# Preparation of a state-space filter: its reciprocals spread over more rounds, its low parts on another engine, and a longer pace

## The chip, the cores and the metric

The kernel runs on one core of a Trainium2 chip. The core has TensorE (matmuls, written to PSUM; PE in the profile), VectorE (DVE), ScalarE (ACT), GpSimd (POOL) and SyncE (SP), which mostly issues DMAs. Each engine takes its own instructions strictly in the order of its queue and waits for others by semaphores. The metric is device time in microseconds. Three runs of the kernel before took 731.43 us in the median (729.15 to 732.84).

## The reference

The input `u` is 2048 tokens of 448 channels. It is normalised per token, and three things are added up: the input itself, a long convolution of the normalised input (one filter per channel, given by 256 complex exponentials), and a gated unit with 1792 hidden units.

```python
x = A_u
xn = _layernorm(x, axis=-1)
return x + _A_ref(xn, ...) + _B_ref(xn, B_w_gate, B_w_up, B_w_down)

# _A_ref: filter K from log_A_real, A_imag, C_real, C_imag, log_dt, then a convolution
dt = jnp.exp(log_dt)
A = -jnp.exp(log_A_real) + 1j * A_imag
C = (C_real + 1j * C_imag) * dt[:, None]
P = jnp.exp((A * dt[:, None])[:, :, None] * pos[None, None, :])
K = 2.0 * jnp.einsum("dn,dnl->dl", C, P).real
y = irfft(rfft(u_t, 2 * L) * rfft(K, 2 * L), 2 * L)[:, :, :L]     # plus u * D_skip

# _B_ref
h = sigmoid(x @ w_gate) * (x @ w_up)
return h @ w_down
```

## The kernel before

Two Python generators emit the program side by side: `conv()` for the convolution and `glu()` for the gated unit. Each `yield` gives a number of units; a loop always advances the generator that has done the smaller share of its `total`. So the numbers `WP`, `WX`, `WK`, `WS` and `HOLE` set how much of the gated unit is emitted beside each stretch of the convolution. The order of emission gives priorities to a scheduler, which lays out each engine's queue by a timeline of its own; `hp(...)` raises a priority and `tc.issue_after(...)` keeps an instruction behind another.

The gated unit works in fp32 split in two parts (high and low, type `fp32r`). A slice is one of 14 blocks `f` of 128 hidden units and one of two tiles `t` of 512 tokens of a half; the halves of the tokens come one after the other. A slice has 22 matmuls into two PSUM banks `gu` (L705), a tanh on ScalarE (`th`, L713), `hf` on VectorE, which frees the second bank (L716), its high part `hh` on ScalarE (L721) and low part `hl` on VectorE (L723). In the first half each block also has its weights split: `wh` on ScalarE (L756), `wl` on VectorE (L760), `dh` on ScalarE (L786), `dl` on GpSimd (L787). After two or three blocks come eight groups of matmuls `po` of two or three blocks (L817), each added to `acc` by VectorE (an eviction, L822). `gu` and `po` share four PSUM banks, in turn.

The convolution's head loads and normalises the first 1024 tokens and then prepares the filter's parameters. `prep(pool, h, srcs)` is a generator that handles half the channels (112 partitions, 512 elements); two of them (h = 0, 1) are stepped in turn, one step each per round, with `yield WP` after a round. Its steps:

- the exponential of `log_A_real` and `log_dt` (`exp`, L297 to L310: mostly VectorE),
- modulus and angle of C: the larger part `m3` (L348), its reciprocal in four pieces of 128 (`pieces(m3)`, L314), quotient `w3`, then ScalarE's sign and arctan (L350 to L357),
- 1/(1 + tanh) as `pl`, again `pieces(pl)`, and from it `W1` by transposes on TensorE into `ko` and `kp` (`turn`, L427),
- sine and cosine of the angle, the phases U, V and T (L378 to L404), each in a high part (`high`, ScalarE, L387) and a low part (`low`, GpSimd, L394), all stored to DRAM by `keep` (SP's queue, L383),
- the factors `a3`, `b3` (L411 to L415), turned into `GG`.

In rounds 2 and 3 the loop also emits eight first-stage blocks of the tokens' spectra (`x_spec`: matmuls L278 into `tr`, a copy on ScalarE L289, stores on SP L292). These matmuls are kept behind the newest gated-unit matmul in emission.

Then `kgen` makes the filter in 56 steps of 8 channels: phases loaded back from DRAM into `ph` (`phase_load`, L482), a matmul into `tr` (L532), sines on ScalarE (L540 to L543), magnitudes `me`, `mf` on GpSimd (L498, L510) with powers `pm` on VectorE (L446), the products `Et` and `Ft` on VectorE (L597 to L599), and 64 small matmuls `ko` (L613). Last come the products of the spectra and the way back (`spectra`, from L839), emitted beside the rest of the gated unit.

Of the kernel before, what the change touches and what calls it, by code (L numbers as in the profile page):

```python
# [15 lines left out]
ALU = mybir.AluOpType  # L16
# [5 lines left out]
N = 256  # L22
# [6 lines left out]
NFT = F // 128  # L29
WK = 5.5  # L30
WS = 4.5
HOLE = 6
WS = 4.5
WP = 5
WX = 2
HELD = 9
HP = 300
Y0 = (8, 1)
# [12 lines left out]
NCK = D // DC  # L51
# [77 lines left out]
def s4d_glu_kernel(ctx, tc, io):  # L129
    nc = tc.nc  # L130
    hp = tc.high_priority
    v = nc.vector
# [138 lines left out]
    def row(b, g):  # L271
        return 32 * (b // 4 % 2) + 8 * g + 4 * (b // 8) + b % 4

    def x_first_stage(to, xn, g):

        s = slice(32 * g, 32 * g + 32)
        for i in range(2):
            nc.tensor.matmul(to[64 * i : 64 * i + 64], wx[s], xn[i][s], start=True, stop=True)  # L278

    def x_spec(xn, b0):  # L280

        for p in range(2):
            x1 = slots[("x1a", "x1b", "x1c")[x1s[0] % 3]]
            x1s[0] += 1
            ps = psc[-1].tile([128, 2, 512], F32, name="tr", bufs=1)
            with tc.issue_after(glu_mm[0].ins):
                for j in range(2):
                    x_first_stage(ps[:, j, :D], xn, 2 * p + j)
            nc.scalar.copy(x1, ps[:, :, :D])  # L289
            for i in range(2):  # L290
                r = row(b0 + i, 2 * p)
                nc.sync.dma_start(x1_d[:, r : r + 9 : 8], x1[64 * i : 64 * i + 64])  # L292
            yield WX

    def exp(ex, ki, fr, pl):

        v.tensor_scalar(ex, ex, lim[:CP, 0, 1:2], lim[:CP, 0, 2:3], ALU.min, ALU.max)  # L297
        yield
        nc.scalar.activation(ki, ex, AF.Identity, scale=1.0 / math.log(2.0))
        yield  # L300
        ln2h = 0.693359375
        ln2l = math.log(2.0) - ln2h
        v.scalar_tensor_tensor(fr, ki, -ln2h, ex, ALU.mult, ALU.add)
        v.scalar_tensor_tensor(fr, ki, -ln2l, fr, ALU.mult, ALU.add)
        cs = [1.0 / math.factorial(i) for i in range(8)]
        v.tensor_scalar(pl, fr, cs[7], None, ALU.mult)  # L306
        for i in range(6, 0, -1):
            v.scalar_tensor_tensor(pl, pl, cs[i], fr, ALU.add, ALU.mult)
        v.tensor_scalar(ki, ki, 127.0, 8388608.0, ALU.add, ALU.mult)
        v.scalar_tensor_tensor(ex, pl, 1.0, ki.bitcast(F32), ALU.add, ALU.mult)  # L310

    def pieces(t):
        for i in range(0, 2 * N, 128):
            v.reciprocal(t[:, i : i + 128], t[:, i : i + 128])  # L314


    SF = [CP, 2 * N]
# [15 lines left out]
    def prep(pool, h, srcs):  # L333

        cr, ci, aim, ex = srcs
        new = lambda n, sh=SF, dt=F32: pool.tile(sh, dt, name=n, bufs=2)
        a3, b3, m3, w3, s3 = (new(n) for n in ("a3", "b3", "m3", "w3", "s3"))
        ki, fr, pl = new("ki", [CP, 2 * N + 2], I32), new("fr", [CP, 2 * N + 2]), new("pl", [CP, 2 * N + 2])
        hdt = pool.tile([CP, 2], F32, name="hdt", bufs=2)
        part = lambda t, i: t[:, N * i : N * i + N]  # L340
        dt = lambda i: ex[:, 2 * N + i : 2 * N + i + 1]

        nc.scalar.activation(a3, cr, AF.Abs, scale=lim[:CP, 0, 0:1])
        nc.scalar.activation(b3, ci, AF.Abs, scale=lim[:CP, 0, 0:1])
        yield from exp(ex, ki, fr, pl)
        v.tensor_scalar(hdt, ex[:, 2 * N :], 0.5, None, ALU.mult)
        yield
        v.scalar_tensor_tensor(m3, a3, 1e-37, b3, ALU.max, ALU.max)  # L348
        pieces(m3)
        v.tensor_tensor(w3, a3, b3, ALU.min)  # L350
        v.tensor_tensor(w3, w3, m3, ALU.mult)
        v.tensor_tensor(s3, a3, b3, ALU.subtract)
        nc.scalar.activation(s3, s3, AF.Sign)
        nc.scalar.activation(cr, cr, AF.Sign)
        nc.scalar.activation(w3, w3, AF.Arctan)
        if h == 1:
            nc.scalar.activation(junk[:CP], w3[:, 0:1], AF.Silu)  # L357
        yield

        fr, pl, ki = fr[:, : 2 * N], pl[:, : 2 * N], ki[:, : 2 * N]  # L360
        for i in range(2):
            nc.scalar.activation(part(fr, i), part(ex, i), AF.Tanh, scale=hdt[:, i : i + 1])
        nc.scalar.activation(pl, fr, AF.Identity, bias=one[:CP])
        pieces(pl)
        v.scalar_tensor_tensor(pl, fr, -2.0, pl, ALU.mult, ALU.mult)
        yield
        turn(pl, W1s[0], h)
        v.scalar_tensor_tensor(w3, w3, -math.pi / 4, s3, ALU.add, ALU.mult)
        nc.scalar.activation(m3, w3, AF.Sin, bias=qpi[:CP])
        nc.scalar.activation(s3, w3, AF.Sin, scale=-1.0, bias=qpi[:CP])  # L370
        v.scalar_tensor_tensor(w3, w3, -math.pi / 4, cr, ALU.add, ALU.mult)
        nc.scalar.activation(w3, w3, AF.Identity, bias=hpi[:CP])
        v.tensor_scalar(ci, ci, 0.0, -2.0 / TWO_PI, ALU.is_lt, ALU.mult)
        v.scalar_tensor_tensor(w3, ci, 1.0 / TWO_PI, w3, ALU.add, ALU.mult)
        yield

        for i in range(2):
            v.tensor_scalar(part(fr, i), part(aim, i), 1.0 / TWO_PI, dt(i), ALU.mult, ALU.mult)  # L378
        nc.scalar.copy(ki, fr)
        U, V, T = aim, fr, w3  # L380
        def keep(d, i, src):
            rows = d[2 * CP * h : 2 * CP * h + 2 * CP].rearrange("(t p) i n -> p t i n", t=2)
            nc.sync.dma_start(rows[:, :, i], three(src).bitcast(F32))  # L383

        def high(i, src):
            hi = slots[f"P{i}"][:, h]
            nc.scalar.copy(hi, src)  # L387
            keep((phu_d, phv_d, phv_d)[i], (0, 0, 1)[i], hi)
            if i:
                keep(phh_d, i - 1, hi)  # L390

        def low(i, src):
            lo = src.bitcast(F32R)
            nc.gpsimd.tensor_tensor(lo, src, slots[f"P{i}"][:, h], ALU.subtract)  # L394
            keep((phu_d, phv_d, phv_d)[i], (1, 3, 2)[i], lo)

        v.tensor_tensor(U, fr, ki, ALU.subtract)
        nc.scalar.activation(ki, U, AF.Identity, scale=64.0)
        v.scalar_tensor_tensor(w3, U, 31.5, w3, ALU.mult, ALU.add)
        yield  # L400
        v.scalar_tensor_tensor(V, U, -64.0, ki, ALU.mult, ALU.add)
        v.scalar_tensor_tensor(w3, V, 0.5, w3, ALU.mult, ALU.add)
        nc.scalar.copy(ki, w3)
        v.tensor_tensor(T, ki, w3, ALU.subtract)  # L404
        for i, src in enumerate((U, V, T)):
            high(i, src)
        for i, src in enumerate((U, V, T)):
            low(i, src)
        yield

        v.tensor_tensor(a3, a3, s3, ALU.mult)  # L411
        v.tensor_tensor(b3, b3, m3, ALU.mult)
        v.tensor_tensor(a3, a3, b3, ALU.add)
        for i in range(2):
            v.tensor_scalar(part(a3, i), part(a3, i), 2.0, dt(i), ALU.mult, ALU.mult)  # L415
        yield
        turn(a3, GGs[0], h)
        yield
# [598 lines left out]
    def conv():  # L1017
        with tc.tile_pool(name="psk", bufs=1, space=PSUM) as ps_, tc.tile_pool(
# [9 lines left out]
            with tc.tile_pool(name="pst", bufs=1, side="right", reuse_waits="tile") as pst:  # L1028
# [18 lines left out]
                xns = []  # L1047
# [34 lines left out]
                n = 0  # L1082
                while preps:
                    for p in list(preps):
                        try:
                            with tc.issue_after(hfs[max(0, len(hfs) - LAG)].ins):
                                next(p)
                        except StopIteration:
                            preps.remove(p)
                    yield WP  # L1090
                    n += 1
                    if n in (2, 3):
                        if n == 2:
                            slots["x1c"] = pst.tile([128, 2, D], F32, name="x1c", tag="raw1")
                        for b in range(0, 4, 2):
                            yield from x_spec([xns[n - 2][:, b + i] for i in range(2)], 4 * (n - 2) + b)
            with tc.tile_pool(name="pk", bufs=1, side="right", reuse_waits="tile") as pk:
                yield from kgen(pk)
        yield HOLE
# [8 lines left out]
    xq, psc, raws, acl, marks, slots, pqs = list(x_first), [], [], [], [None, None], {}, []  # L1108
    W1s, GGs, act = [], [], []
    gens = [conv(), glu()]  # L1110
    total = [sum(Y0) + 11 * WP + 8 * WX + 14 + NCK * WK + HOLE + 17 * WS, 2 * (4 + NFT * 14.8) - HELD]
    done = [0.0, 0.0]
    done[0] += next(gens[0])
    held = False
    while any(g is not None for g in gens):
# [3 lines left out]
        i = min(live, key=lambda i: done[i] / total[i])  # L1119
# [33 lines left out]
```

## Time and profile before

| what | value |
|---|---|
| median of three runs | 731.43 us (729.15 to 732.84) |
| the profiled execution's own time | 734.12 us |
| its span, first to last instruction | 732.3 us |
| mean granted TensorE clock | 0.973 |
| DMA | 116.76 MB, mean 159 GB/s |

The profile is of one execution, whose time is the span and 1.8 us around it. Lines of it are read like this: a line of the timeline has start, length, engine, line of the kernel (L705), operation, output and input by the program's names, shape and count, and in brackets how long the engine was idle before it and what ended that. Matmul durations overlap, since they are pipelined; the distance from start to start is what one costs. "SPq" and "ACTq" are DMA issues on SP and ScalarE.

### The profile page before, as it was taken

How to read it: one execution, taken by the hardware profiler on the slowest of the kernel's cores; microseconds unless marked ns; L12 is line 12 of the kernel's file. 1: busy time of each engine (PE TensorE's matmuls, PEld its weight loads, DVE VectorE, ACT ScalarE, POOL GpSimd, SP SyncE). 2: the span in 40 equal slices, each digit the busy share in tenths (PEclk: the TensorE clock that was granted, in tenths of full speed). 3: DMA queues.
4: the chain of work that ended last, by engine and by line, in shares of the span. 5: the costliest groups of instructions: out<-in, count | busy, mean ns of one | idle time of the engine just before them, and what ended most of it. 6: DMA issues, size and time to landing. Idle time of an engine off the chain costs nothing.

```text
span 732.3 us, 19070 instructions
## 1 busy us (share of the span) xinstructions
PE 680.6 (93%) x7780; PEld 535.8 (73%) x7780; DVE 567.3 (77%) x776; ACT 420.8 (57%) x650; POOL 377.3 (52%) x423
## 2 busy tenths in 40 slices
PE   2898799997998999999999999999999999989994
PEld 1665688786876887566878887888877787766783
DVE  5799996799989999998498988986955555654553
ACT  3646364678587778997388678768633312313310
POOL 2120027799887788786557856767843003251001
PEclk9998899999999999997999999999999999999998
DMA  9946328435314544553952322232359999999756
GB/s 202 227 111 199 80 82 276 146 104 186 126 51 154 176 155 136 157 151 120 267 179 98 93 97 96 76 102 96 70 160 294 265 233 239 217 227 250 178 138 162
DMA packets 93287, 116.76 MB, mean 159 GB/s; under 512 B 12177, under 2 KB 81169, under 8 KB 92945
## 3 DMA queue, kind: packets, MB, share of 16 engines
q1 hardware_dynamic: 83888, 95.08, 48.1%
q10 hardware_dynamic: 6736, 14.57, 6.3%
q0 software_dynamic: 2576, 5.90, 3.3%
q8 instruction: 61, 1.00, 0.6%
q14 instruction: 26, 0.20, 0.1%
HBM read 70.75 MB, written 44.76 MB: 158 GB/s over the span
## 4 chain that ended last, share of the span: by engine, by line
PE 60%; DVE 17%; DMA 6%; ACT 6%; issue 5%; SPq 3%; POOL 1%; ACTq 0%; DVEq 0%; POOLq 0%
PE gu L705 23%; PE po L817 15%; PE sp L899 7%; PE ko L613 6%; PE pv L926 4%; PE tr L532 3%; DVE Ft L599 2%; DVE Et L598 2%; DVE Et L597 2%; DVE hl L723 2%; DMA acc_d<-acc 1%; DMA sx<-x_d 1%; DVE wl L760 1%; DVE hf L716 1%; PE kq L558 1%
## 5 line engine op out<-in xcount | busy, mean ns | idle before, releaser
L510 POOL TENSOR_TENSOR me<-me,pm 128x32 f32<-128x32 f32 (+1 forms) x168 | 144.4, 860 | 88.4 <-DVE Et L598 76.3
L510 POOL TENSOR_TENSOR mf<-mf,pm 128x64 f32<-128x64 f32 (+1 forms) x112 | 119.5, 1067 | 4.9
L705 PE MATMUL gu<-xh,wh 128*128 128x512 f32 x336 | 101.1, 407 | 3.0 <-ACT xh L218 2.8
L705 PE MATMUL gu<-xh,wl 128*128 128x512 f32 x336 | 96.1, 394 | 0.0
L705 PE MATMUL gu<-xl,wh 128*128 128x512 f32 x336 | 95.1, 390 | 0.0
L817 PE MATMUL po<-dh,hh 128*128 128x448 f32 x224 | 86.6, 387 | 3.3 <-DVE acc L822 2.5
L597 DVE TENSOR_TENSOR Et<-me,S 128x1024 f32<-128x1024 f32 x56 | 81.6, 1457 | 8.0 <-ACT S L543 4.1
L598 DVE TENSOR_TENSOR Et<-me,S 128x1024 f32<-128x1024 f32 x56 | 79.8, 1425 | 8.2 <-ACT me L523 5.8
L599 DVE TENSOR_TENSOR Ft<-mf,S 128x1024 f32<-128x1024 f32 x56 | 78.9, 1408 | 7.3 <-ACT S L543 4.4
L817 PE MATMUL po<-dl,hh 128*128 128x448 f32 x224 | 84.3, 376 | 0.0
L817 PE MATMUL po<-dh,hl 128*128 128x448 f32 x224 | 83.6, 375 | 0.0
L540 ACT ACTIVATE S<-tr 128x1024 f32<-128x1024 f32 x56 | 57.7, 1030 | 42.7 <-PE tr L532 37.4
L721 ACT CAST hh<-hf 128x512 fp32r<-128x512 f32 x56 | 35.0, 626 | 80.4 <-DVE hf L716 62.8
L705 PEld LDWEIGHTS gu<-xh,wh 128*128 128x128 f32 x336 | 61.8, 191 | 21.7 <-ACT xh L218 4.2
L705 PEld LDWEIGHTS gu<-xh,wl 128*128 128x128 f32 x336 | 63.3, 189 | 15.2 <-DVE pl L306 0.7
L613 PEld LDWEIGHTS ko<-Et,Ft 128*32 128x32 f32 x3584 | 54.1, 111 | 27.4 <-issue 16.6
L705 PEld LDWEIGHTS gu<-xl,wh 128*128 128x128 f32 x336 | 63.1, 188 | 14.1 <-issue 0.7
L613 PE MATMUL ko<-Et,Ft 128*32 128x64 f32 x3584 | 64.2, 222 | 9.0 <-DVE Et L597 4.6
L716 DVE SCALAR_TENSOR_TENSOR hf<-th,gu 128x512 f32<-128x512 f32 x56 | 38.1, 681 | 36.4 <-PE gu L705 27.3
L822 DVE SCALAR_TENSOR_TENSOR acc<-po,acc 128x448 f32<-128x448 f32 x80 | 48.5, 615 | 22.8 <-PE po L817 22.7
L543 ACT ACTIVATE S<-S,hpi 128x1024 f32<-128x1024 f32 x56 | 65.6, 1171 | 0.0
L723 DVE TENSOR_TENSOR hl<-hf,hh 128x512 fp32r<-128x512 f32 x56 | 48.9, 874 | 16.6 <-ACT hh L721 16.6
(196 smaller groups left out, 1293.9 us busy)
## 6 DMA issues: line engine op xcount, KB each, us to landing
sk_d<-sk ACTq DMA_DIRECT2D x14, 512.0 KB
sx<-x_d SPq DMA_DIRECT2D x32, 224.0 KB
skl<-sk_d SPq DMA_DIRECT2D x16, 448.0 KB
vp<-v_d SPq DMA_DIRECT2D x16, 448.0 KB
v_d<-vt SPq DMA_DIRECT2D x62, 112.0 KB
wt_d<-wh SPq DMA_DIRECT2D x9, 512.0 KB
wt_d<-wl SPq DMA_DIRECT2D x9, 512.0 KB
wl<-wt_d SPq DMA_DIRECT2D x9, 512.0 KB
```

The lines of the kernel that those rows point to most:

```text
L510: ins = nc.gpsimd.tensor_tensor(m[:, :, w + a : 2 * w : n], m[:, :, a:w:n], par(base + i).unsqueeze(2).to_broadcast([128, 4 * DC, w // n]) ...
L540: nc.scalar.activation(rows(cs), pv, AF.Abs)
L543: sins[:] = [nc.scalar.activation(cs, cs, AF.Sin, scale=-TWO_PI, bias=hpi)]
L597: v.tensor_tensor(Et[:, :, :, 32:64], two(me[:, :, 32:64]), S[:, 1::-1], ALU.mult)
L598: v.tensor_tensor(Et[:, :, :, 0:32], two(me[:, :, 0:32]), S[:, 1:3, :, ::-1], ALU.mult)
L599: fts[:] = [v.tensor_tensor(Ft, two(mf), S[:, 3:5], ALU.mult)]
L613: nc.tensor.matmul(ko[32 * j : 32 * j + 32, sl], Ft[:, cc, DC * h + 4 * q + j], Et[:, cc, DC * h + 4 * q + j], start=(k == 0), stop=(k == ...
L705: glu_mm[:] = [nc.tensor.matmul(ps, a_, b_, start=(n == 0), stop=(n == len(mm) - 1))]
L723: v.tensor_tensor(hl, hf, hh, ALU.subtract)
L817: glu_mm[:] = [nc.tensor.matmul(po, a_[:, bs], w_, start=(n == 0), stop=(n == 3 * fc - 1))]
L822: v.scalar_tensor_tensor(acc[:, b], po, 0.5, acc[:, b], ALU.mult, ALU.add)
L899: mm = nc.tensor.matmul(to, tb[:kk, t, 64 * c : 64 * c + 64], rhs, start=True, stop=True, skip_group_check=True,)
```

## The change

The diff, line numbers as in the file before:

```diff
-WP = 5
+WP = 70 / 19
@@
-    def pieces(t):
-        for i in range(0, 2 * N, 128):
-            v.reciprocal(t[:, i : i + 128], t[:, i : i + 128])
+    def pieces(t, h):
+
+        for i in range(4):
+            if i // 2 == h:
+                for o in (256 * (i % 2), 256 * (i % 2) + 128):
+                    v.reciprocal(t[:, o : o + 128], t[:, o : o + 128])
+            yield
@@ prep
-        pieces(m3)
+        yield from pieces(m3, h)
@@ prep
-        pieces(pl)
+        yield from pieces(pl, h)
@@ prep, low
-            nc.gpsimd.tensor_tensor(lo, src, slots[f"P{i}"][:, h], ALU.subtract)
+            v.tensor_tensor(lo, src, slots[f"P{i}"][:, h], ALU.subtract)
@@ conv, the loop over preps
-                    if n in (2, 3):
-                        if n == 2:
+                    if n in (3, 5):
+                        if n == 3:
                             slots["x1c"] = pst.tile([128, 2, D], F32, name="x1c", tag="raw1")
                         for b in range(0, 4, 2):
-                            yield from x_spec([xns[n - 2][:, b + i] for i in range(2)], 4 * (n - 2) + b)
+                            yield from x_spec([xns[n // 5][:, b + i] for i in range(2)], 4 * (n // 5) + b)
@@
-    total = [sum(Y0) + 11 * WP + 8 * WX + 14 + NCK * WK + HOLE + 17 * WS, 2 * (4 + NFT * 14.8) - HELD]
+    total = [sum(Y0) + 19 * WP + 8 * WX + 14 + NCK * WK + HOLE + 17 * WS, 2 * (4 + NFT * 14.8) - HELD]
```

- Each call of `pieces` now takes four steps. The first half of the channels does its four reciprocals in the first two, two in each; the second half in the last two. With two calls, preparation has 19 rounds where it had 11.
- A round counts 70/19 = 3.68 units where it counted 5, so all rounds count 70 where they counted 55. The convolution's total goes from 484.5 to 499.5 units, the gated unit's stays at 413.4.
- The six low parts of the phases (three for each half of the channels, 112 by 512) are subtracted by VectorE and no longer by GpSimd.
- The spectrum blocks are emitted after rounds 3 and 5, four after each.

Nothing else is changed, and the arithmetic is the same.

## The prediction

> **What bounds the kernel now.** I read the page's shares and slices first, then a table of stages, then TensorE's and VectorE's timelines up to the first products of the filter.
>
> ```profile
> PE 680.6 (93%) x7780; PEld 535.8 (73%) x7780; DVE 567.3 (77%) x776; ACT 420.8 (57%) x650; POOL 377.3 (52%) x423
> PE   2898799997998999999999999999999999989994
> DVE  5799996799989999998498988986955555654553
> PEclk9998899999999999997999999999999999999998
> ```
>
> ```profile
> 57.50:89.20 31.70, 24.14 (x108) 17.20 (x108) 29.96 (x51) 17.02 (x25) 0.20 (x1) 0.78 0.53 152
> 89.20:137.70 48.50, 47.24 (x224) 40.00 (x223) 37.08 (x57) 25.34 (x48) 23.33 (x24) 1.00 0.57 177
> 137.70:311.00 173.30, 164.52 (x2375) 130.97 (x2373) 165.02 (x164) 137.39 (x203) 146.07 (x145) 0.98 0.42 135
> 345.00:546.00 201.00, 198.70 (x3005) 163.41 (x3005) 161.82 (x168) 139.33 (x201) 133.12 (x154) 1.00 0.40 122
> 546.00:732.30 186.30, 172.74 (x1394) 131.30 (x1392) 98.40 (x188) 45.04 (x86) 35.50 (x45) 0.98 0.91 217
> ```
>
> First the shares and 40 equal slices of the span in tenths, then stages: length, then busy time of PE, PEld, DVE, ACT and POOL, granted clock, share of DMA, GB/s. TensorE bounds the whole (93%), and after 345 us nearly all of it (198.70 of 201.00). Two stages are different. In 57.5 to 89.2 it stands idle 7.6 us at a granted clock of 0.78 while VectorE works 29.96 of 31.70: here preparation and the gated unit share VectorE's queue. In 137.7 to 311 both are at 95%: TensorE by its pipelined records, VectorE by real work. So the change can gain in the first of these, and whether the gain lasts is settled in the second.
>
> The hole itself, on TensorE and then on VectorE (start, length, instruction, what it waited for), and two runs of matmuls from the chain of waits:
>
> ```profile
> 59.61 0.98 PE L278 MATMUL tr<-xn,wx 32*64 32x448 f32 x8 [1.07 <-ACT x1ab L289]
> 61.66 1.77 PE L278 MATMUL tr<-xn,wx 32*64 32x448 f32 x8 [1.07 <-ACT x1ab L289]
> 64.23 0.74 PE L817 MATMUL po<-dh,hh 128*128 128x448 f32 x1 [0.80 <-DVE hf L716]
> 64.77 0.57 PE L817 MATMUL po<-dl,hh 128*128 128x448 f32 x1
> 65.15 0.58 PE L817 MATMUL po<-dh,hl 128*128 128x448 f32 x1
> 75.48 0.98 PE L278 MATMUL tr<-xn,wx 32*64 32x448 f32 x8 [2.10 <-ACT x1ab L289]
> 78.98 0.74 PE L817 MATMUL po<-dh,hh 128*128 128x448 f32 x1 [2.52 <-DVE acc L822]
> 89.17 0.86 PE L705 MATMUL gu<-xh,wh 128*128 128x512 f32 x3
> ```
>
> ```profile
> 42.42 0.69 DVE L716 SCALAR_TENSOR_TENSOR hf<-th,gu 128x512 f32<-128x512 f32 x1 [0.45 <-ACT th L713]
> 47.93 0.68 DVE L716 SCALAR_TENSOR_TENSOR hf<-th,gu 128x512 f32<-128x512 f32 x1
> 56.31 5.00 DVE L314 RECIPROCAL m<-m 112x128 f32<-112x128 f32 x6
> 61.22 1.16 DVE L760 TENSOR_TENSOR wl<-wraw,wh 128x1024 fp32r<-128x1024 f32 x1
> 62.30 1.28 DVE L308 SCALAR_TENSOR_TENSOR pl<-pl,fr 112x514 f32<-112x514 f32 x2
> 63.50 0.68 DVE L716 SCALAR_TENSOR_TENSOR hf<-th,gu 128x512 f32<-128x512 f32 x1
> 77.10 0.68 DVE L723 TENSOR_TENSOR hl<-hf,hh 128x512 fp32r<-128x512 f32 x1
> 78.31 1.68 DVE L822 SCALAR_TENSOR_TENSOR acc<-po,acc 128x448 f32<-128x448 f32 x3
> 89.92 3.38 DVE L314 RECIPROCAL pl<-pl 112x128 f32<-112x128 f32 x4
> 96.92 0.63 DVE L716 SCALAR_TENSOR_TENSOR hf<-th,gu 128x512 f32<-128x512 f32 x1
> ```
>
> ```profile
> 89.33 10.04 PE gu L705 x44
> 708.93 9.31 PE po L817 x45
> ```
>
> The second `po` needs the PSUM bank that the fifth `hf` frees; `hf` at 63.50 stood behind six reciprocals (5.00 us) and a `wl`. Then matmuls start 0.38 us apart (64.77, 65.15) where a warm `po` takes 9.31/45 = 0.207 us (a gate matmul 10.04/44 = 0.228). The fifth `po` waits again, for an eviction at 78.31. Prices on VectorE, start to start, read from here: 0.84 us a reciprocal (3.38/4), 0.60 an operation of 512 (62.30 to 63.50 for two), 1.1 a `wl`, 0.55 an eviction (1.68/3).
>
> **The change, part by part.** I have the changed program's instructions as they stand in each queue, and followed them with these prices. In the queue the steps of two are not kept: the reciprocals of `m` stand four and four, with an `hl`, two steps of the exponential, a tiny one and the fourth `hf` between; those of `pl` stand eight in a row.
>
> To the fourth slice. Four steps of the exponential (2.4 us) now stand ahead of the second tile's low parts; the third `hf` comes at about 44.7, was 42.42. The fourth stands behind two `m3`, a `wl` and four reciprocals: about 54.4, was 47.93. TensorE still has gate matmuls queued, so this costs it about 1 us.
>
> The fifth `hf`. Behind the fourth, ending at 55.0, are four reciprocals (3.35), eight operations of 512 (4.8: two pairs `w3` and `s3`, two products of `w3` and `m3`, two of four steps of the exponential), the other two of those steps (1.2), `wl` (1.1), `hl` (0.6) and two tiny steps (0.4): 66.5, was 63.50. ScalarE's two signs wait for `s3` at 59.6 and 60.8, and the copy of a spectrum block is queued behind them, so TensorE has only 0.9 us of work between 59.6 and 67.1, with stalls of 2.8 and 3.9 us around it. That is the longest stall of the new order, and I let 15 matmuls after it run cold: 15 x (0.375 - 0.207) = 2.5 us, as in the old one.
>
> The evictions. The sixth `hl` is at about 72.9 (was 77.10), because the powers of the exponential are done, and the first eviction at 73.9 (was 78.31). Then `pl` exists, and eight reciprocals (6.7 us, 74.8 to 81.5) stand ahead of the other seven evictions; the fifth `po` starts at about 82.1, and 27 `po` and a last spectrum block later the gates of f = 3 start at about 88.0, was 89.17. **Gain 1.2 us.** What the reciprocals cost here is hidden for all but 1.5 us by two `po` and two spectrum blocks that need none of those banks; with `pl` 2 us later they would cost 2 us more.
>
> f = 3 to 5. The old queue used 89.9 to 96.7 for reciprocals, and the seventh `hf` came at 96.92, 2.7 us after its gate. In the new one VectorE waits for that gate until 93.3, about 8 us idle, and after it come 21.1 us of preparation (30 operations of 512, of which six are the moved low parts, and ten short ones) with 8.8 us of the gated unit: it ends at about 123.2. The low parts, on GpSimd before:
>
> The first fence is GpSimd's line by itself, the second VectorE's groups up to 145 us (busy us, mean ns, idle before), the third the timeline.
>
> ```profile
> L394 POOL TENSOR_TENSOR aim<-aim,p x2: 2818/3152/3487, 106.0 to 112.0; 112x512 fp32r<-112x512 f32 x2
> L394 POOL TENSOR_TENSOR w<-w,P x2: 1286/1294/1302, 117.8 to 120.6; 112x512 fp32r<-112x512 f32 x2
> ```
>
> ```profile
> L402 DVE SCALAR_TENSOR_TENSOR w<-fr,w 112x512 f32<-112x512 f32 x2 | 2.5, 1230 | 0.0
> L404 DVE TENSOR_TENSOR w<-ki,w 112x512 f32<-112x512 int32 x2 | 2.8, 1409 | 0.0
> L399 DVE SCALAR_TENSOR_TENSOR w<-aim,w 112x512 f32<-112x512 f32 x2 | 1.4, 680 | 0.0
> ```
>
> ```profile
> 123.06 0.54 SPq L383 DMA_DIRECT2D phv_d<-w  x1
> 128.99 0.42 SPq L482 DMA_DIRECT2D ph<-phv_d  x1
> 131.56 0.70 PE L532 MATMUL tr<-sel,ph 128*128 128x512 f32 x2 [1.26 <-DMA ph<-phv_d]
> 137.67 0.87 PE L705 MATMUL gu<-xh,wh 128*128 128x512 f32 x3
> 143.90 0.67 DVE L716 SCALAR_TENSOR_TENSOR hf<-th,gu 128x512 f32<-128x512 f32 x1
> 144.88 1.10 PE L613 MATMUL ko<-Et,Ft 128*32 128x64 f32 x64
> ```
>
> Six at 0.60 are 3.6 us more for VectorE. Against it, operations beside the old ones took twice their time (`L402` 1230 ns and `L404` 1409 against 680 for `L399`, two each): 2.6 us, most of it given back. The phases don't come earlier: the last low part ends at 123.2 instead of 121.9 (120.6 and 1.3), its store is issued some 0.6 us later, and between it and the fourth load of `ph` SP issues nearly the same list (5.9 us from 123.06 to 128.99). So `ph` lands at about 131.5 as before, but nothing waits for it: TensorE's first `tr` now stands behind the first gate of f = 6. TensorE, fed throughout but for 0.4 us, begins f = 6 at about 134.6, was 137.67, of which 0.5 is that `tr`. **Gain 2.5 us for TensorE.**
>
> VectorE has no such gain. Hand-followed, it has at 144.9 done what it had before at 143.90 (thirteenth `hf`, first `Et` and `Ft`): 1.0 us behind.
>
> The pace and the blocks at rounds 3 and 5. Weighed by the two prices, gated-unit matmuls ahead of the first `ko` in TensorE's queue grow from 96.3 to 104.0 us, so that `ko` stands at about 150.0 (144.88); ahead of the 24th they are 196.9 in both, ahead of the last 338.9 and 341.4, and from the fifth step of the spectra on equal. So 7.7 us of matmuls leave the stage in which both engines are at 95%. The eight spectrum blocks all still precede f = 3; their stores are read only after 546, and cost nothing.
>
> The sum, from 137.7 on. If TensorE paces, its 2.5 us stay: -2.5. If VectorE paces, +1.0. I take the middle, -0.8, since both rows say 95%. After 345 TensorE carries either on. In the spectra 2.5 us of filler are gone and the DMA share is 0.91 on average; TensorE has 172.74 of 186.30 there, so I count nothing, at worst +2.5. The profiled execution took 734.12 us (span 732.3 and 1.8 around it), 2.7 above the median 731.43; -0.8 on each is 733.3 and **730.6**.
>
> **The rivals.** *Warm matmuls, shorter hole (faster).* The two cold stretches of the old order cost about 2.5 us each. If the stall before 67.1 is broken up by the spectrum block in time and the later ones stay short, no stretch is cold: 2.5 more, and with TensorE pacing 2.5 + 2.5 = 5.0, 726.4. For it: 75.48 was warm after 2.10 us of idle. Against it: 61.66 was cold after two gaps of 1.07 us (0.98 and 1.77 for the same eight matmuls). The Trainium skill (TensorE: Matmul & The Clock Gate, on what's actually happening) has the clock halve after an idle window of about 3.4 us; by it my stall of 3.9 us is cold, but one a little shorter would not be. The cold 61.66 agrees poorly with that.
>
> *VectorE paces to 345 (slower).* Place: 137.7 to 311, VectorE 165.02 of 173.30. The first `ko` is 5.1 us later, and 7.7 us of gated unit take only about a third of that from VectorE (a slice of 7.5 us of matmuls costs it 0.60 + 0.60 + 0.55 + 0.73 = 2.5): 2.6 us. So the 24th `ko` comes 2.5 us later, and with the spectra's 2.5 us not made up the end is 5.0 later: 736.4. It decides once VectorE doesn't idle at all from the first `Et` on; the 8.3 us it idles there now speak against a pure case.
>
> *The steps don't part the reciprocals, and the head is no better.* The queue already shows eight in a row. If `pl` is ready 3 us later than I have it, the fifth `po` is later by 3, and gain and loss cancel: 731.4 or a little above. This ends in the forecast's class.
>
> **How the numbers follow.** Faster by over 0.5% means under 727.8, slower over 735.1 (0.5% is about what a measurement of this kernel can tell from no change). Forecast with the cancelling case: 0.42. Warm rival and other gains: 0.32, since every one of the head's steps that I followed has more room above than below once the second stall goes. VectorE rival: 0.26. The forecast's own range is 728 to 734; a scheduler has put some 600 later instructions in another order, which no row prices, so I reach past both rivals by 2 to 3 us: 723.5 to 738.5.
>
> **What would show it.** Right: a fifth `hf` at 65 to 68 with TensorE idle before it; the first eviction near 74 and the next after a run of eight reciprocals; gates of f = 3 at 87 to 89, of f = 6 at 133 to 136; low parts of 0.6 us on VectorE; first `Et` 2 to 4 us later; VectorE still about 95% to 311. Wrong: f = 3 under 85 or over 91, a first `Et` more than 6 us later, or a stall over 3 us in the second half.

## The result, and the profile after

| | before | after |
|---|---|---|
| median of four runs each | 732.13 us | 751.57 us |
| lowest and highest | 729.15, 735.36 | 749.45, 756.11 |
| profiled execution, its span | 734.12, 732.3 | 749.45, 747.7 |
| mean granted clock of that execution | 0.973 | 0.970 |

After over before is 1.0273, 95% interval 1.0208 to 1.0338: slower, by some 20 us. The profile of after is of its fastest run, so the traces explain 15.4 us of span.

The page after, in the rows shown of before (shares; then busy tenths in 40 slices):

```profile
PE 685.3 (92%) x7780; PEld 536.5 (72%) x7780; DVE 567.7 (76%) x782; ACT 421.2 (56%) x650; POOL 347.9 (47%) x417
...
PE   2896899998999899979989999999899999989994
...
DVE  5798689699989998996489888888964555564553
...
PEclk9998999999999999998999999999899999999997
```

The table of stages (length; busy PE, PEld, DVE, ACT, POOL; granted clock, DMA share, GB/s):

```profile
57.50:89.20 31.70, 21.77 (x105) 15.14 (x104) 26.34 (x47) 16.55 (x25) 1.60 (x2) 0.84 0.56 161
89.20:137.70 48.50, 47.70 (x226) 40.53 (x225) 39.22 (x72) 24.73 (x47) 10.58 (x13) 1.00 0.58 176
137.70:311.00 173.30, 165.12 (x2298) 131.25 (x2296) 155.93 (x160) 133.29 (x196) 137.50 (x147) 0.97 0.41 131
345.00:546.00 201.00, 192.77 (x2852) 156.91 (x2853) 165.03 (x169) 139.48 (x202) 130.60 (x160) 0.98 0.37 117
546.00:747.70 201.70, 189.00 (x1758) 145.22 (x1756) 106.01 (x197) 54.05 (x99) 40.75 (x50) 0.97 0.86 213
```

VectorE's own total hardly moved (567.3 to 567.7). In 57.5 to 89.2 TensorE has less work done than before (21.77 against 24.14), so the hole of the head isn't smaller. And 345 to 546, where TensorE was busy 198.70 of 201, now has 8.23 us of idle TensorE: a stage that the prediction held for settled.

To see where the time goes, I took for the same instructions the end in the one trace less the end in the trace before. `hf` counts the gates and `Ft` the filter's steps, in VectorE's order; us, positive is later. e1 to e15 are the experiments of the next section. One of e13's seven executions, the profiled one, ran at a granted clock of 0.746 and took 856.22 us, so e13 has no row here and its time below is that of the other six.

```
                     Ft1  Ft25  hf25  hf34  hf41  hf48  hf56  span
time in before     142.5 316.0 283.3 396.2 490.2 555.9 692.4 732.3
after               +8.1  +6.3  +0.3  +6.3  +7.9 +16.7 +15.2 +15.4
e1 pace             -1.4  -0.5  -3.2  +0.1  +1.5 +10.2  +6.9  +6.8
e2 steps            +2.2  -0.4 +13.4 +14.2 +14.1 +14.1 +12.6 +12.3
e3 low parts        +0.1  +0.3  -2.2 +10.5 +11.4 +11.3  +9.8 +10.1
e4 steps + low      -3.2 -10.5  +4.3  +3.1  +3.8  +3.8  -0.5  -0.6
e5 after, reload    +9.7 +12.6  +4.1  +8.9  +9.8 +17.1 +16.0 +16.2
e6 before, reload   -0.8  +1.2  +0.5  -1.0  -0.3  -0.2  -1.4  -1.2
e7 low, reload      -0.3  +1.3  -1.7  +7.6  +7.8  +7.9  +6.4  +6.5
e8 steps + pace     +8.4  +3.8  -1.9  +3.7  +4.8 +13.8 +10.4 +10.2
e9 after, paid back+12.8  +6.0 +17.5 +16.7 +17.4 +17.4 +15.3 +15.3
e10 pace, paid back -3.6  -3.7  -4.0  -0.1  -0.2  -0.2  -1.5  -1.7
e11 before, late    -6.3  +1.2  -0.9  +1.4  +2.8 +11.4  +9.5  +9.6
e12 steps+low, late -4.3  +0.2  -1.4  +2.4  +3.9 +11.6  +9.1  +9.3
e14 pace, masks     +2.1  +2.0  -0.9  +2.7  +4.4 +16.8 +17.5 +17.5
e15 after, paid late+10.5 +8.4  +2.4  +7.8 +12.2 +13.4 +13.2 +14.1
```

The row of after has two jumps: 6.3 us by the 34th gate, and 8.8 between the 41st and the 48th. The first begins in the head, as a filter that is 8.1 us late (Ft1); the second is far behind every instruction that the diff touches.

### The profile page after: what moved, and what is told of

It is laid out like the page before. It is cut to its first block, busy times and chain, and to the rows that moved or that the text cites. A ratio compares the mean times of both kernels' runs of the same rounds, so it can differ in the third digit from the quotient of the medians.

```text
span 747.7 us, 19077 instructions
## 1 busy us (share of the span) xinstructions
PE 685.3 (92%) x7780; PEld 536.5 (72%) x7780; DVE 567.7 (76%) x782; ACT 421.2 (56%) x650; POOL 347.9 (47%) x417
## 4 chain that ended last, share of the span: by engine, by line
PE 64%; DVE 17%; DMA 7%; ACT 4%; issue 4%; SPq 2%; ACTq 1%; POOL 1%; DVEq 0%; POOLq 0%
PE gu L709 25%; PE po L821 14%; PE sp L903 7%; PE ko L617 7%; PE pv L930 4%; PE tr L536 3%; DVE Ft L603 3%; DVE Et L601 2%; DVE Et L602 2%; DMA acc_d<-acc 2%; DVE hl L727 1%; DMA acc<-in_A_u_dram 1%; DVE wl L764 1%; DMA wraw<-in_B_w_up_dram 1%; PE kp L562 1%
## 5 line engine op out<-in xcount | busy, mean ns | idle before, releaser
L514 POOL TENSOR_TENSOR me<-me,pm 128x32 f32<-128x32 f32 (+1 forms) x168 | 135.0, 803 | 89.0 <-DVE Et L602 81.7
L514 POOL TENSOR_TENSOR mf<-mf,pm 128x64 f32<-128x64 f32 (+1 forms) x112 | 117.3, 1048 | 5.2
L602 DVE TENSOR_TENSOR Et<-me,S 128x1024 f32<-128x1024 f32 x56 | 85.5, 1527 | 12.7 <-ACT me L527 11.9
L603 DVE TENSOR_TENSOR Ft<-mf,S 128x1024 f32<-128x1024 f32 x56 | 80.5, 1438 | 10.7 <-ACT S L547 5.1
L601 DVE TENSOR_TENSOR Et<-me,S 128x1024 f32<-128x1024 f32 x56 | 82.3, 1471 | 7.5 <-ACT S L547 7.0
L617 PEld LDWEIGHTS ko<-Et,Ft 128*32 128x32 f32 x3584 | 57.1, 114 | 32.6 <-DVE Ft L603 14.0
L617 PE MATMUL ko<-Et,Ft 128*32 128x64 f32 x3584 | 68.3, 228 | 13.3 <-DVE Ft L603 11.6
L717 ACT ACTIVATE th<-gu 128x512 f32<-128x512 f32 x56 | 33.7, 602 | 48.9 <-PE gu L709 48.8
```

What stands on the lines that cost most here:

```text
L514: ins = nc.gpsimd.tensor_tensor(m[:, :, w + a : 2 * w : n], m[:, :, a:w:n], par(base + i).unsqueeze(2).to_broadcast([128, 4 * DC, w // n]) ...
L601: v.tensor_tensor(Et[:, :, :, 32:64], two(me[:, :, 32:64]), S[:, 1::-1], ALU.mult)
L602: v.tensor_tensor(Et[:, :, :, 0:32], two(me[:, :, 0:32]), S[:, 1:3, :, ::-1], ALU.mult)
L603: fts[:] = [v.tensor_tensor(Ft, two(mf), S[:, 3:5], ALU.mult)]
L617: nc.tensor.matmul(ko[32 * j : 32 * j + 32, sl], Ft[:, cc, DC * h + 4 * q + j], Et[:, cc, DC * h + 4 * q + j], start=(k == 0), stop=(k == ...
```

## The experiments

All ratios are against the kernel before, run beside them on the same chip.

| run | median, us | ratio (95% interval) |
|---|---|---|
| e1 pace alone | 742.3 | 1.0102 (1.0039 to 1.0166) |
| e2 steps alone | 745.5 | 1.0148 (1.0095 to 1.0201) |
| e3 low parts alone | 745.1 | 1.0151 (1.0103 to 1.0199) |
| e4 steps and low parts | 733.3 | 0.9988 (0.9959 to 1.0017) |
| e5 after, reload moved | 751.2 | 1.0277 (1.0246 to 1.0309) |
| e6 before, reload moved | 732.3 | 0.9999 (0.9975 to 1.0024) |
| e7 low parts, reload moved | 740.7 | 1.0112 (1.0076 to 1.0149) |
| e8 steps and pace | 746.3 | 1.0219 (1.0174 to 1.0264) |
| e9 after, pace paid back | 750.4 | 1.0225 (1.0162 to 1.0288) |
| e10 pace alone, paid back | 731.9 | 1.0001 (0.9971 to 1.0030) |
| e11 before, late order | 742.7 | 1.0125 (1.0079 to 1.0170) |
| e12 e4 with late order | 742.5 | 1.0127 (1.0089 to 1.0165) |
| e13 after, masks later | 756.0 | 1.0357 (1.0320 to 1.0393) |
| e14 pace alone, masks later | 746.4 | 1.0224 (1.0191 to 1.0257) |
| e15 after, pace paid back late | 746.0 | 1.0215 (1.0185 to 1.0244) |

### The parts one by one (e1 to e4, e8)

Theory A: the longer pace costs, the rest is harmless. Theory B: the work added to the head costs. e1 has the pace alone (`WP = 70 / 11` for 11 rounds), e3 the low parts alone. e2 has the new `pieces` with the blocks after rounds 3 and 5, and 55 units in all; e4 is e2 with the low parts; e8 is e2 with 70 units.

```diff
# e1
-WP = 5
+WP = 70 / 11
# e2, with pieces as in the change; e8 has 70 / 19
-WP = 5
+WP = 55 / 19
# e3, and e4 on top of e2
-            nc.gpsimd.tensor_tensor(lo, src, slots[f"P{i}"][:, h], ALU.subtract)
+            v.tensor_tensor(lo, src, slots[f"P{i}"][:, h], ALU.subtract)
```

> Only the pace of the changed kernel, on the kernel before: 11 rounds that count 70 units together instead of 55; reciprocals and low parts as before. Theory A (the pace costs): in the changed kernel the filter's steps stand 14.5 to 16.5 us behind those of before from the 29th on (19.4 us in the median); the longer pace puts the queue from the 26th step on in the changed kernel's order, so with it alone the time is 742 to 750 us and the filter's steps are about 10 us or more late in the second half. Theory B (the head costs: reciprocals and low parts make the first Ft 8.2 us late, and the pace is harmless): 728 to 736 us, the first Ft within 3 us of 142.5.

> Only the reciprocals in steps of two with the spectrum blocks after rounds 3 and 5, on the kernel before; 19 rounds that count 55 units together, low parts on GpSimd. Theory A (the pace costs): 728 to 736 us, the later order is that of before. Theory B (the head costs): 738 to 745 us, since the head has the changed order of reciprocals, and the first Ft later than 142.5 by 4 us or more. In the queue the first ko stands behind 88.0 us of gated-unit matmuls instead of 96.4; if TensorE is as well fed as before, it comes 8 us earlier.

> Only the six low parts on VectorE, on the kernel before. Theory A (the pace costs): within 0.5% of before, 728 to 736 us. Theory B with the low parts at fault: 736 to 740 us, as 3.6 us of VectorE's time are added before the filter starts and the 2.6 us that GpSimd's work took from its neighbours don't come back.

> The changed kernel with the pace put back: reciprocals in steps and low parts on VectorE, 19 rounds that count 55 units together. Theory A (the pace costs): 727 to 736 us, so that nearly all of the 19 us is gone. Theory B (the head costs): 742 to 750 us, nearly all of it still there.

Neither theory holds as put. e1 and e4 came out as A says, but steps alone and low parts alone cost 1.5% each and nothing together. Parts that cancel when joined aren't prices of instructions. Their places differ, too: e2 has lost its 13 us by the 25th gate (9.6 of them by the ninth, which stands in the head), e3 loses 12.7 us between the 25th and the 34th, at the crossing of the halves. So I looked at the crossing, and at whether parts add. e8, run with the next three, joins steps and pace:

> The steps with the pace of 70 units; low parts left on GpSimd. The parts add up only if they work by themselves: pace 1.0102 times steps 1.0148 is 1.0252, so 751 us. If the order that the scheduler draws decides (theory D), anything between 733 and 760 us may come, and its filter's first tr must stand behind more matmuls of the gated unit than in the kernel before (101 us of them ahead of the first ko, 96 before).

This pair may simply add: 1.0252, the product of e1 and e2, lies inside the interval of 1.0219. But its loss isn't where e2 has it. The 25th gate is on time (-1.9), and its row has after's two jumps: 3.7 us by the 34th gate, 9.0 from the 41st to the 48th.

### The crossing of the halves (e5 to e7)

At the crossing ScalarE issues the reload of two accumulators, and these issues wait for the store of the old ones. ScalarE's waits from 345 to 385 us (us in total, times, longest), first in the kernel after, then in the kernel before:

```profile
ACT hh L725 <- DMA acc_d<-acc: 9.5, 1, 9.5
```

```profile
ACT hh L721 <- DMA acc_d<-acc: 4.2, 1, 4.2
```

Theory C: this wait is the loss. The edit takes the loads to GpSimd's queue, in after (e5), before (e6) and e3 (e7):

```diff
-                    x_load(accs[q], 4 * q, 4, [nc.scalar])
+                    x_load(accs[q], 4 * q, 4, [nc.gpsimd])
```

> The changed kernel, with the reload of the accumulators at the crossing of the halves (eight loads of acc, which wait for the store acc_d<-acc to land) issued from GpSimd's queue and no longer from ScalarE's. Theory C, the crossing costs: in the changed kernel's trace the cast hh at 372.97 us stood idle for 9.46 us behind these loads, in the trace before for 4.23 us. Without it the changed kernel gains 5 to 10 us: 742 to 747 us. Theory A, the pace of the head costs and what is lost at the start stays lost to the end: within 2 us of 751.6 us.

> The kernel before, with the same edit (the reload on GpSimd's queue) and nothing else. Theory C: 2 to 5 us less than before, since 4.23 us of ScalarE's wait go: 728 to 731 us. Theory A: unchanged, 732 us, since there the wait is covered.

> Low parts on VectorE alone, with the reload on GpSimd's queue; TensorE's order is that of the low parts alone, matmul for matmul. Theory C: the 8.72 us in which ScalarE stood behind the reload are this kernel's whole loss, so it comes back to the kernel before: 732 to 737 us. Theory A or B: stays at 745 us.

C fell for the change: e5 is as slow as after, and e6 as fast as before. In e5 the wait did go, and two others stand at the place, behind VectorE. ScalarE's waits in e5, same stretch:

```profile
ACT pm L453 <- DVE pm L450: 4.0, 1, 4.0
ACT S L544 <- DVE acc L826: 3.6, 1, 3.6
```

At most it holds for a part of e3: e7's ratio is 0.4% lower, with intervals that overlap, and 2.9 us fewer are lost by the 34th gate.

The table suggests what the crossing does instead. In after, e1, e8 and e11 the lag of the 34th gate is within 0.6 us of the filter's lag at Ft25; in e2 and e9, where the gates are much later than the filter, it is within 0.8 of that of the 25th gate. So the two streams seem to meet there, with the later one setting the lag. Of the others, e4, e6, e14 and e15 follow this to within 2.2 us and e5, e10 and e12 to within 4 only, and e3 and e7 don't: their loss arises at the crossing itself. It is a reading of the table, which no run tested by itself.

### The second jump: a later order (e9 to e12)

The merge gives the streams their turns by shares of each one's total, so fifteen units more for the head shift the filter against the gated unit to its last step. In all kernels with 70 units TensorE's queue is nearly the same from the 28th `ko` on (212.1 us of gated-unit matmuls ahead of it, by the two prices of the prediction), and in all with 55 it is the queue of before (204.6). Theory E: this late order holds the 8.8 us. Rival F: all of it is lost in the head. "Paid back" takes the fifteen units off again where the filter starts; "late" puts them in there and not in the head:

```diff
# e9 on after, e10 on e1 (total with 55 units)
-        yield 14
+        yield 14 - 15
# e11 on before, e12 on e4 (total with 70 units)
-        yield 14
+        yield 14 + 15
```

> The changed kernel, in which the fifteen units that the head's pace adds are taken off again at the filter's start (yield 14 - 15, total with 55), so that TensorE's order is the changed kernel's up to the first ko and the one of the kernel before from the 28th ko on. Theory E: the longer pace also puts the work of 490 to 556 us in another order, in which VectorE is held twice by GpSimd (two Et of 3.43 and 5.89 us in the place of 1.2), and that costs about 8 us in every kernel with 70 units; so this one takes 740 to 745 us, and its 48th hf is no later against the kernel before than its 41st. Rival F, all that is lost is lost in the head and kept to the end: 749 to 753 us.

> The pace of 70 units alone, taken off again in the same way. Theory E: 732 to 737 us, about the kernel before. Rival F: as the pace alone, 740 to 744 us.

> The kernel before with the fifteen units put in at the filter's start and not in the head: TensorE's order in the head nearly that of before, and from the 28th ko on the changed kernel's. Theory E: 738 to 743 us, with the two long Et between 490 and 556 us. Rival F: 731 to 735 us.

> Steps and low parts with 55 units in the head (733 us by themselves) and the fifteen put in at the filter's start: from the 28th ko on the changed kernel's order. Theory E: 738 to 743 us, with the two long Et. Rival F: 732 to 735 us.

E holds three times over: paid back, the pace costs nothing (e10, 1.0001); the late order alone costs 1.25% (e11), with or without the steps and low parts (e12), and 8.6 of e11's 9.6 us lie between the 41st gate and the 48th. In e9 too the second jump is gone (17.4 at the 41st gate and at the 48th). But e9 is not clearly faster than after (1.0225 and 1.0273, with intervals that overlap), since its first term grew from 6.3 to 16.7 us: with the filter late and its steps now due earlier, the gates fall behind instead (hf25 +17.5). There E's sum was wrong.

What the late order does. VectorE and GpSimd in the kernel after; the `acc` at 533.02 is an eviction that the next down projections need:

```profile
520.45 3.43 DVE L602 TENSOR_TENSOR Et<-me,S 128x1024 f32<-128x1024 f32 x1
...
527.21 5.89 DVE L602 TENSOR_TENSOR Et<-me,S 128x1024 f32<-128x1024 f32 x1
533.02 0.61 DVE L826 SCALAR_TENSOR_TENSOR acc<-po,acc 128x448 f32<-128x448 f32 x1
...
519.46 3.34 POOL L772 TENSOR_TENSOR wl<-wraw,wh 128x1024 fp32r<-128x1024 f32 x1
...
526.89 0.32 POOL L514 TENSOR_TENSOR me<-me,pm 128x64 f32<-128x64 f32 x1
...
530.97 1.05 POOL L514 TENSOR_TENSOR me<-me,pm 128x512 f32<-128x512 f32 x1
```

An `Et` undisturbed takes 1.2 us. The first one ends 1.08 us after GpSimd's `wl` (523.88 and 522.80). The second starts at 527.21, as the first of nine masks ends that GpSimd ran back to back, and ends 1.08 us after the last of them (533.10 and 532.02). No semaphore is named; it looks as if VectorE got to read only when GpSimd was done. The chain of waits of after runs through it, and the window shows what it costs TensorE (both of after; chain: start, us, what):

```profile
527.28 5.82 DVE Et L602
533.10 0.53 DVE acc L826
```

```profile
530.00:540.00 10.00, 6.63 (x82) 5.33 (x81) 10.00 (x9) 1.88 (x3) 7.01 (x8) 0.77 0.08 22
540.00:550.00 10.00, 10.00 (x102) 7.70 (x101) 6.58 (x8) 6.60 (x10) 1.76 (x4) 0.89 0.44 113
```

TensorE is idle for 3.4 us, and the clock of 0.77 and 0.89 takes up to 2.3 and 1.1 us more (an estimate: the share of each 10 us that wasn't granted, a part of which falls into the idle time): 6.8 at most. By the 44th gate after is 7.5 us late, by the 45th 15.1. The same pair of `Et` stands in e1, e5, e8, e11 and e12, all with the late order, within 0.3 us of the same lengths, and in no kernel whose late order is that of before. The same 40 us in the kernel before, then in e1, then in e10, which is e1 paid back:

```profile
520.00:560.00 40.00, 39.33 (x513) 30.99 (x502) 26.02 (x33) 17.64 (x29) 20.28 (x25) 1.00 0.68 182
```

```profile
520.00:560.00 40.00, 35.99 (x548) 29.14 (x539) 28.28 (x25) 18.59 (x27) 20.98 (x29) 0.91 0.37 107
```

```profile
520.00:560.00 40.00, 39.33 (x499) 31.13 (x496) 26.03 (x33) 17.45 (x29) 20.95 (x25) 1.00 0.69 194
```

The Trainium skill (SBUF — State Buffer, on who interferes with whom) has a VectorE instruction with two SBUF inputs contend with a GpSimd instruction that reads SBUF. It says of VectorE's two-port modes that whoever issues first gets the shared pair of ports for the whole instruction and the other is blocked, and in general that issue order decides who blocks. The first `Et` agrees with that: `wl` had started 0.99 us earlier (519.46 and 520.45). The second goes further than one instruction: VectorE stood through the eight masks that were left of the run.

### Is it the masks, and do the two terms add? (e13 to e15)

e13 (on after) and e14 (on e1) make GpSimd wait with those masks: a copy of one element reads the 54th `Ft`, and the masks are queued behind it. TensorE's order is kept but for the last two products. e15 pays the fifteen units back at the 37th product.

```diff
# e13, e14: the masks of steps 55 and 56, and their squares on ScalarE
-                    if c % 2 == 1:
+                    if c % 2 == 1 and cn != 53:
                         squares(coming[0])
...
-                if cn + 2 < NCK and c % 2 == 0:
+                if cn == 53:
+                    dmy = const.tile([128, 1], F32, name="dmy")
+                    mls[:] = [nc.gpsimd.tensor_copy(dmy, Ft[:, 0, 0, 0:1])]
+                    coming = magnitudes(27)
+                    squares(coming[0])
+                if cn + 2 < NCK and c % 2 == 0 and cn != 52:
# e15
+                if cn == 36:
+                    total[0] -= 15
+                    yield -15
```

> The changed kernel, in which GpSimd builds the masks of the filter's last two steps (eleven me and mf) only after the 54th Ft, held there by a one-element copy that reads Ft; in the changed kernel they run from 527 to 532 us, just while the Et of 5.89 us stands on VectorE. TensorE's order is the changed kernel's but for the last two products. Theory G: VectorE is held by GpSimd's run of masks, and the eviction acc and the down projections behind it: the Et of 5.89 us goes, the jump of 7.5 us between the 44th and the 45th hf falls to under 3.5 us, and 4 to 6 us are gained: 745 to 748 us. Rival H, it is the order of TensorE that costs there: 750 to 753 us.

> The pace of 70 units alone, with the same edit of the last masks. Theory G: 736 to 739 us. Rival H: 741 to 744 us.

> The changed kernel, with the fifteen units taken off after the crossing of the halves, at the 37th product of the filter: TensorE's order is the changed kernel's up to there and, from the 48th product on, nearly the one of the kernel before. If the loss is two terms, 6.3 us that the 34th hf shows already and 8.8 us between the 41st and the 48th, the first stays and the second goes: 738 to 741 us, the lag of the 34th hf still 5 to 8 us. If the two are one (what is not lost at the one place is lost at the other, as with the fifteen units taken off at the filter's start): 748 to 752 us.

Both G and H missed the times. e14 is slower than e1, from which it was made; e13's ratio is above that of after, with intervals that just overlap. The trace of e14 says why (VectorE's timeline, then GpSimd's first late mask and a later `wl`):

```profile
523.67 1.21 DVE L598 TENSOR_TENSOR Et<-me,S 128x1024 f32<-128x1024 f32 x1
524.80 0.61 DVE L827 SCALAR_TENSOR_TENSOR acc<-po,acc 128x448 f32<-128x448 f32 x1
...
542.19 1.65 DVE L599 TENSOR_TENSOR Ft<-mf,S 128x1024 f32<-128x1024 f32 x1 [3.99 <-POOL mf L510]
543.76 4.08 DVE L598 TENSOR_TENSOR Et<-me,S 128x1024 f32<-128x1024 f32 x2
547.77 4.49 DVE L597 TENSOR_TENSOR Et<-me,S 128x1024 f32<-128x1024 f32 x2
...
535.53 0.32 POOL L498 TENSOR_TENSOR mf<-GG,pm 128x64 f32<-128x64 f32 x1
...
546.84 3.20 POOL L773 TENSOR_TENSOR wl<-wraw,wh 128x1024 fp32r<-128x1024 f32 x1
```

The `Et` of 5.89 us is down to 1.21, and from the 44th to the 45th gate e14 loses 1.2 us (4.0 to 5.2) where e1 loses 7.3 (1.2 to 8.5). So the masks do cause the hold, and the hold that jump. But the masks are now late themselves: an `Ft` waits 3.99 us for them, TensorE 4.6 us for an `Et`, and from the 45th gate to the 46th e14 loses 8.6 us. That `Et` had a hold of its own: the first of the pair at 547.77 took 3.36 us and ended 1.09 us after the `wl` that GpSimd had begun at 546.84. The stall moved and grew.

e15 came between its two expectations: 1.0215. The 34th gate is 7.8 us late as in after, no `Et` is held, and the second jump is 1.2 us (12.2 to 13.4); but 4.4 us are lost between the 34th gate and the 41st, the stretch in which the filter's steps move up. So the jump goes with the late order, but taking it away gives back less than its size: e15's trace is 1.3 us shorter than that of after, and its ratio 0.6% lower, with intervals that overlap.

## Why the prediction was wrong, point by point

**The fifth `hf` at 66.5: right, and by the path forecast.** It started at 67.01, and TensorE stood idle 2.74 and 3.67 us around one spectrum block (2.8 and 3.9 forecast). The kernel after, in the head (timeline of VectorE, then of ScalarE and TensorE, and a window of the clock):

```profile
67.01 0.67 DVE L720 SCALAR_TENSOR_TENSOR hf<-th,gu 128x512 f32<-128x512 f32 x1
...
74.27 1.23 DVE L764 TENSOR_TENSOR wl<-wraw,wh 128x1024 fp32r<-128x1024 f32 x1 [2.48 <-ACT wh L760]
...
75.59 0.69 DVE L727 TENSOR_TENSOR hl<-hf,hh 128x512 fp32r<-128x512 f32 x1
...
76.48 0.62 DVE L826 SCALAR_TENSOR_TENSOR acc<-po,acc 128x448 f32<-128x448 f32 x1
...
77.09 6.63 DVE L317 RECIPROCAL pl<-pl 112x128 f32<-112x128 f32 x8
...
73.19 1.05 ACT L760 CAST wh<-wraw 128x1024 fp32r<-128x1024 f32 x1 [3.12 <-DMA wraw<-in_B_w_up_dram]
...
63.09 0.98 PE L278 MATMUL tr<-xn,wx 32*64 32x448 f32 x8 [2.74 <-ACT x1ab L289]
67.74 0.74 PE L821 MATMUL po<-dh,hh 128*128 128x448 f32 x1 [3.67 <-DVE hf L720]
...
84.25 0.47 PE L821 MATMUL po<-dh,hh 128*128 128x448 f32 x1 [2.10 <-DVE acc L826]
...
91.44 0.86 PE L709 MATMUL gu<-xh,wh 128*128 128x512 f32 x3
```

```profile
84.79:88.20 3.41, 3.41 (x11) 3.02 (x10) 1.62 (x3) 0.00 (x0) 0.00 (x0) 0.50 0.40 121
```

**The evictions, "gain 1.2 us": wrong.** The sixth `hl` was put at 72.9 and the first eviction at 73.9; they came at 75.59 and 76.48. I had counted what VectorE must do, not when its input is there: a `wl` ahead of that `hl` waits 2.48 us for `wh`, and `wh` 3.12 us for a weight load. The eight reciprocals cost what was said (6.63 for 6.7), and the other evictions came after them, so the fifth `po` started at 84.25, not at 82.1. From there to f = 3 it took 7.2 us instead of 5.9: the granted clock was 0.50 from 84.79 to 88.20, and the forecast had no cold matmuls there. So f = 3 starts at 91.44, not 88.0, and the gain of 1.2 is a loss of 2.3. "Wrong: f = 3 over 91" was one of the signs.

**f = 3 to 5, "gain 2.5 us for TensorE": wrong, mostly by what was lost ahead of it.** The stage took 47.5 us (46.6 forecast, 48.5 before), so f = 6 starts at 138.98 instead of 134.6; 3.4 of these 4.4 us are the late f = 3. After again, at the filter's start (VectorE, SP, TensorE):

```profile
126.57 0.68 DVE L398 TENSOR_TENSOR w<-w,P 112x512 fp32r<-112x512 f32 x1
...
144.76 0.69 DVE L720 SCALAR_TENSOR_TENSOR hf<-th,gu 128x512 f32<-128x512 f32 x1 [4.72 <-PE gu L709]
146.21 1.30 DVE L601 TENSOR_TENSOR Et<-me,S 128x1024 f32<-128x1024 f32 x1 [0.76 <-ACT S L547]
...
131.36 0.68 SPq L387 DMA_DIRECT2D phv_d<-w  x1
...
137.00 0.43 SPq L486 DMA_DIRECT2D ph<-phv_d  x1
...
138.98 0.86 PE L709 MATMUL gu<-xh,wh 128*128 128x512 f32 x3
...
141.50 0.63 PE L536 MATMUL tr<-sel,ph 128*128 128x512 f32 x2
...
154.37 1.10 PE L617 MATMUL ko<-Et,Ft 128*32 128x64 f32 x64
```

The low parts do take 0.6 to 1.0 us on VectorE. The last starts at 126.57 (its end was forecast at 123.2). Its store is issued at 131.36, 4.1 us after it ends and 8.3 us later than before where 0.6 was forecast, because other stores and weight loads stand ahead of it on SP. From there to the fourth load of `ph` it is 5.64 us, about as forecast (5.9). The first `tr`, at 141.50, didn't wait for that load, so this lateness doesn't show in its start.

**VectorE 1.0 us behind: right for the gates by luck, wrong for the filter.** The thirteenth `hf` is 0.86 later, but not because VectorE was busy up to it: VectorE stood idle 4.72 us for its gate, since f = 6 was late. With the first `Et` and `Ft` it was to be done at 144.9, and was at 150.6. The first `Et` was to start 2 to 4 us later than before, and started 7.4 us later (146.21); the first `Ft` ended 8.1 us later. That the first `tr` stands behind a gate of f = 6 was in the forecast; that f = 6 starts 4.4 us late was not. The first `Et` in the kernel before:

```profile
138.81 1.23 DVE L597 TENSOR_TENSOR Et<-me,S 128x1024 f32<-128x1024 f32 x1 [2.17 <-DMA wt_d<-wl]
```

The first `ko` is at 154.37 instead of 150.0 (144.88 before): the 7.7 us of matmuls moved ahead of it came as computed, and no gain of the head stood against them.

**"After 345 TensorE carries either on": this step failed most.** The prediction said that some 600 later instructions stand in another order, "which no row prices". It widened the range by 2 to 3 us for that and put nothing into the sum, with TensorE busy 198.70 of 201 us there. That order costs 1.25% by itself (e11), about 9 us, nearly all at one place, where VectorE stands behind GpSimd. This is the step that failed: a new order of the work of VectorE and GpSimd, put at nothing in the sum, holds a stall of TensorE that the old order did not have. A busy share of 99% says that the old order had no stall there, not that another order has none. "A stall over 3 us in the second half" had been listed as a sign.

**The rivals.** *VectorE paces to 345* had the right sign and not the mechanism: VectorE was busy 155.93 of 173.30 us from 137.7 to 311, less than before, and did not pace. *Warm matmuls* came to nothing: the clock was 0.84 for 0.78 in the hole, which got longer, and matmuls ran cold after the stall that ends at 67.74 and again after the one that ends at 84.25. *The steps don't part the reciprocals* is true (eight in a row), and the lateness that it asked for came, from `wl` and not from `pl`.

**The sum.** Forecast -0.8; measured +15.4 in the traces, 19.4 in the medians. By kernels: steps and low parts together 0.9988 (e4); with the late order 1.0127 (e12); with the fifteen units in the head as well 1.0273. On the old head the same fifteen units add nothing to the late order (e1 1.0102, e11 1.0125). So the last 1.4% goes with the pace and the new head together: 104 us of gated-unit matmuls ahead of the first `ko`, where e1 has 96.6 and e12 94.8, a filter 8.1 us late, and 6.3 us at the crossing. How the late filter becomes the 6.3 us is the reading of the table above, and not shown by a run of its own.

What stays open: why steps alone and low parts alone cost 1.5% each and cancel, and what else than the reload holds e3 at the crossing. No version tried beats the kernel before; e4, e6 and e10 equal it.

## What to carry to other kernels

A cost in a planner (here: units of pace) is a change to every instruction behind it: compare the queues to the end, and price the new order where it differs by what VectorE and GpSimd would then do at the same time, even where TensorE is 99% busy. In a head that is followed by hand, put beside each operation the arrival of its input, weight loads too. Try the parts of a joined change singly and together: 1.5% and 1.5% made nothing here, and a moved stall (e9, e14) came back as large or larger elsewhere.

## What the runs showed of the hardware

VectorE was held through the rest of a run of nine GpSimd instructions (an `Et` of 5.89 us for 1.2). It stands at the same place in every kernel with that order and with the masks where they were: 5.88 to 5.90 us in five of them, 5.64 in e5. Behind a single `wl` of GpSimd an `Et` took 3.43 us in those six and in e14. All other `Et` and `Ft` beside GpSimd's masks in the kernel after ran in 1.2 to 2.1 us, while a mask of 128x512 took 1.05 us by itself and up to 2.1 beside them. So either engine can be the one that waits; what decides it here wasn't tried beyond moving the masks away. And TensorE stalls of 2.1 and 1.2 us within 10 us cost up to as much again in granted clock (0.77, then 0.89 over the next 10 us).
